# A recurrent attention and mixture-of-adapters kernel: batches one at a time, whole-tensor loads, five rotating PSUM banks

## The chip, the cores and the metric

The kernel runs on one core of a Trainium2 chip. The metric is device time in microseconds (us), the median of several executions. One execution is also taken by the hardware profiler; its span runs from the first to the last instruction of the program.

## What is computed

Four batches, eight heads, 768 steps, 48 columns per head, all in float32. A gated linear recurrence runs over the steps of each head; its output, seen as 3072 rows of 384, goes through a mixture of eight rank-16 adapters, of which the two with the highest gate logits are used:

```python
for t in range(S):
    state = alpha[:, :, t, :, None] * state + np.einsum('bhd,bhe->bhde', k[:, :, t], v[:, :, t])
    y[:, :, t] = np.einsum('bhd,bhde->bhe', q[:, :, t], state)
...
logits = x @ w_gate                      # x: y as (3072, 384)
topk = np.argpartition(-logits, K, axis=1)[:, :K]      # K = 2
...                                      # w: softmax over the two
    z = x[mask] @ A[e]
    delta[mask] += w[mask, k, None] * (z @ B[e])
return (x + delta).astype(np.float32)
```

## The kernel before, in words

**Units.** The steps are cut into chunks of 128, six for each batch, and a unit u (0 to 23) is one chunk of one batch with all eight heads: 128 rows on the partitions, 384 columns. `_place(u)` gives a unit its batch and chunk. Before, batches go in pairs: units 0, 2, 4 ... are batch 0 and units 1, 3, 5 ... batch 1, then the other two batches, so two recurrences advance in turn.

**Steps of a unit**, each a short function called with u:

- `ln` (ACT, L238): logarithm of alpha, for one unit or a pair of units (`LNS`); `cum` (PE, L244): sums of it over the chunk by a product with a triangle; `exp` (ACT, L255): two activations, exp of the sums and of their negative, into `ex`.
- `kg` (POOL, L260): k and q times those, one multiplication of 128 x 768 into `kgq`; `vb` (POOL, L265): v to bfloat16.
- `tr` (PE, L268): eight transposes of `kgq`; `kq` (ACT, L274): their copy to SBUF; `at` (PE, L280): eight products of k and q into `at_t`; `msk` (DVE, L288): times the causal mask, into `am`.
- `st` (DVE, L294): state of the chunk before, out of PSUM bank `S_t`, times the decay, into `sb`; `kv` (PE, L300): the new state, an identity product of `sb` and four products of k and v. The first chunk of a batch has no old state.
- `av` (PE, L314): the output, from `sb` and from `am`; `ysb` (ACT, L330): its copy into `o_t`.

**Adapters.** `xb` (POOL, even units), `xt` (PE), `xs` (ACT, L345) bring the output in transposed. Then the units go in groups (`GROUPS`, mostly three): `z` (PE) makes adapter products and logits, `gm df ge wu dn w zw` (DVE, L364 to L418) and `gx` (ACT) the two best, their weights and the weighted z, `zt` (PE) and `zs` (ACT) transpose it. `dl` (PE, L431) is the last product of a unit, `o` (DVE, L437; ACT for unit 23) adds it to `o_t`, and `out` stores 192 KB from SP's queue.

**The order** is written out by hand: each token of the string `ORDER` is a step, its unit or group, and for steps that write a rotating PSUM bank the bank's number (`MB` of them). Every engine runs its own steps in that order; so do the DMA queues. Loads stand among them: `Sk.4.2.exp3` is k on SP's ring from unit 4 on, two units, held until exp of unit 3 is done; `Aa.6.2` is alpha on ACT's ring, so it stands in ACT's own instruction stream. `w` loads are the weights. `load` (L150) turns a token into a DMA; one of two units is 384 KB (128 partitions x 16 rows of 192 B). The tiles `a_t`, `kq_t`, `v_t` have `NS` = 6 places, one for each pair of units, and `home` finds them. `cast_weights` (L211) brings the adapter weights to bfloat16 on DVE, at the token `cw`.

PSUM has eight banks: two for `at_t`, two for `S_t` (one for each of the two recurrences under way), four for the rotating `M_t`.

## Time and profile before

| | |
|---|---|
| median of 5 runs | 99.47 us (98.66 to 99.81) |
| the profiled execution | 99.19 us, span 97.5 us |
| busy, of the span | PE 71.8 (74%), DVE 68.0 (70%), ACT 67.2 (69%), POOL 61.2 (63%) |
| moved by DMA | 24.18 MB; HBM read 19.28 MB, written 4.72 MB |
| costliest groups | kg (L261) 24 x 1822 ns; msk (L289) 24 x 1215 ns; exp (L138) 48 x 507 ns; kq (L141) 24 x 593 ns |

PE is TensorE's matmuls and PEld its weight loads, DVE is VectorE, ACT ScalarE, POOL GpSimd, SP SyncE; ACTq and SPq are the DMA issues on the queues of ACT and SP. An idle time in brackets behind a row names what ended it. A slice of the page is a fortieth of the span, 2.4 us, and a digit the busy share in tenths. In the chain, each piece is what the next one waited for. An "x4" is a number of instructions put in one row.

### The profile page before, as it was taken

The page shows a single profiled execution, that of the slowest core. Times are in us where ns is not written, and L with a number is a line of the kernel's source. Part 1 is how long each engine was busy: PE and PEld are TensorE (multiplying, and loading weights), DVE is VectorE, ACT ScalarE, POOL GpSimd, SP SyncE. Part 2 cuts the span into 40 slices and gives each one's busy share as a digit, 9 for nine tenths or more (in the row PEclk, how much of TensorE's full clock was granted, in tenths as well). Part 3 has the DMA queues.
Part 4 walks back from the last instruction along what each step waited for, and adds up shares of the span by engine and source line. Part 5 has one row for each costly group of instructions (what it writes and reads, how often), then busy time and mean ns, then how long its engine had stood idle before and what let it go on. Part 6 is the DMA issues. An engine that isn't in the chain of part 4 may idle for free.

```text
span 97.5 us, 2861 instructions
## 1 busy us (share of the span) xinstructions
PE 71.8 (74%) x1088; PEld 54.8 (56%) x1088; DVE 68.0 (70%) x171; ACT 67.2 (69%) x155; POOL 61.2 (63%) x70
## 2 busy tenths in 40 slices
...
DMA  1999999999999999999999999999999989998553
GB/s 27 245 260 259 260 260 258 260 230 258 282 263 260 260 254 259 257 236 251 248 242 254 261 261 257 260 238 197 260 205 236 254 165 392 330 392 322 189 205 118
DMA packets 103966, 24.18 MB, mean 248 GB/s; under 512 B 100752, under 2 KB 103952, under 8 KB 103952
## 3 DMA queue, kind: packets, MB, share of 16 engines
...
HBM read 19.28 MB, written 4.72 MB: 246 GB/s over the span
## 4 chain that ended last, share of the span: by engine, by line
DMA 24%; DVE 22%; PE 21%; ACT 15%; POOL 8%; issue 5%; ACTq 1%; POOLq 0%; DVEq 0%
DMA kq_t<-in_q_dram 14%; POOL kgq L261 8%; DVE am L289 7%; DMA v_t<-in_v_dram 6%; DVE o_t L441 6%; ACT ex L138 5%; PE M_t L272 4%; ACT kt L141 4%; PE at_t L285 4%; DMA a_t<-in_alpha_dram 4%; PE M_t L246 3%; DVE w L405 2%; PE M_t L343 2%; ACT lg L138 2%; ACT xs L141 2%
## 5 line engine op out<-in xcount | busy, mean ns | idle before, releaser
L261 POOL TENSOR_TENSOR kgq<-kq_t,ex 128x768 bf16<-128x768 f32 x24 | 43.3, 1822 | 12.8 <-ACT xs L141 4.2
L289 DVE TENSOR_TENSOR am<-at_t,mask 128x1024 bf16<-128x1024 f32 x24 | 29.2, 1215 | 16.4 <-PE at_t L285 16.4
L138 ACT ACTIVATE ex<-M_t 128x392 f32<-128x392 f32 (+1 forms) x48 | 21.2, 507 | 3.0 <-PE M_t L250 3.0
L141 ACT COPY kt<-M_t 128x512 f32<-128x512 f32 x24 | 14.2, 593 | 6.8 <-PE M_t L272 6.5
L272 PE MATMUL M_t<-ident,kgq 128*128 128x128 bf16 x192 | 16.2, 234 | 3.6 <-POOL kgq L261 3.6
L266 POOL CAST vb<-v_t 128x384 bf16<-128x384 f32 x24 | 11.8, 506 | 10.5 <-DMA v_t<-in_v_dram 10.5
L141 ACT COPY o_t<-M_t 128x384 f32<-128x384 f32 x25 | 12.4, 495 | 5.5 <-PE M_t L326 4.8
L246 PE MATMUL M_t<-lg,suf 128*128 128x384 bf16 x24 | 8.9, 369 | 9.5 <-ACT lg L138 9.3
L272 PEld LDWEIGHTS <-kgq 128*128 128x128 bf16 x192 | 12.5, 105 | 5.1 <-POOL kgq L261 4.6
L295 DVE TENSOR_TENSOR sb<-S_t,ex 128x384 bf16<-128x384 f32 x20 | 10.8, 547 | 4.3 <-PE S_t L309 4.0
L441 DVE TENSOR_TENSOR o_t<-M_t,o_t 128x384 f32<-128x384 f32 x23 | 12.2, 546 | 1.6 <-PE M_t L434 1.2
L285 PE MATMUL at_t<-kt 48*128 48x128 bf16 x192 | 10.4, 233 | 2.5 <-ACT kt L141 1.9
L138 ACT ACTIVATE lg<-a_t 128x768 bf16<-128x768 f32 (+1 forms) x13 | 10.6, 813 | 2.4 <-DMA a_t<-in_alpha_dram 2.4
L326 PE MATMUL M_t<-vb,am 128*128 128x48 bf16 x192 | 9.1, 187 | 0.9 <-DVE am L289 0.7
L285 PEld LDWEIGHTS <-kt 48*128 48x128 bf16 x192 | 6.0, 99 | 5.8 <-ACT kt L141 3.6
L434 PE MATMUL M_t<-B_all,zs 128*128 128x384 bf16 x24 | 8.2, 356 | 1.2 <-ACT zs L141 1.2
L326 PEld LDWEIGHTS <-am 128*128 128x128 bf16 x192 | 7.3, 99 | 1.8 <-DVE am L289 1.4
L334 POOL CAST xb<-o_t 128x384 bf16<-128x384 f32 x12 | 6.1, 505 | 2.8 <-ACT o_t L141 2.8
L343 PE MATMUL M_t<-ident,o_t 128*128 128x128 f32 x36 | 7.3, 314 | 0.4 <-DVE mx L367 0.3
L141 ACT CAST xs<-M_t 128x384 bf16<-128x384 f32 x12 | 5.9, 494 | 2.3 <-PE M_t L343 2.3
L309 PE MATMUL S_t<-vb,kgq 128*128 128x96 bf16 x80 | 7.4, 220 | 0.1
L247 PEld LDWEIGHTS <-ident 128*128 128x128 bf16 x24 | 2.5, 102 | 8.2 <-issue 8.2
...
## 6 DMA issues: line engine op xcount, KB each, us to landing
...
```

Source lines behind the costliest of these rows:

```text
L138: recent[:] = [nc.scalar.activation(*args, **kw)]
L141: recent[:] = [nc.scalar.copy(*args)]
L246: nc.tensor.matmul(r[:, 0:DM], suf[:, :], t[:, :, 0:D], start=True, stop=True)
L261: nc.gpsimd.tensor_tensor(out=kgq[u % KEEP["kg"]][:, :, :, 0:D], in0=kq_t[u // 2 % NS][:, :, u % 2, :, 0:D], in1=ex[u % KEEP["ex"]][:, :, ...
L266: nc.gpsimd.tensor_copy(out=vbt[u % KEEP["vb"]], in_=home("v", u)[:, u % 2, :, 0:D])
L272: nc.tensor.transpose(t[:, w, p, :], pair(kgq[u % KEEP["kg"]][:, w], p), ident[:, :])
L285: nc.tensor.matmul(at_t[:, hh, p, :], kq[rows, 0, p, :], kq[rows, 1, p, :], start=True, stop=True)
L289: nc.vector.tensor_tensor(out=am[u % KEEP["am"]].rearrange("p a b t -> p (a b) t"), in0=at_t.rearrange("p a b t -> p (a b) t"), in1=_bc_mi ...
L295: nc.vector.tensor_tensor(out=sb[u % KEEP["sb"]].rearrange("p a b d -> p (a b) d"), in0=S_t[u % 2].rearrange("p a b d -> p (a b) d"), in1= ...
L326: nc.tensor.matmul(y[:, h * D:(h + 1) * D], am[u % KEEP["am"]][:, hh, p, :], vbt[u % KEEP["vb"]][:, h, :], start=(c == 0 and h == 0), stop ...
L343: nc.tensor.transpose(t[:, i * P:(i + 1) * P], x[:, i, :], idn[:, :])
L441: nc.vector.tensor_tensor(out=o_t[u], in0=bank("dl", u)[:, 0:DM], in1=o_t[u], op=ALU.add)
```

## The change

- `_place`: units 0 to 5 are batch 0, 6 to 11 batch 1, and so on. One recurrence is under way at a time, with one `S_t` bank; `MB` goes from four to five.
- `load`: a load takes one tensor of one batch whole (six units, 1152 KB; 128 partitions x 48 rows of 192 B), sixteen in all; alpha and q on SP's ring, k and v on ACT's. The tiles hold two batches, with the columns in the order head, chunk. The first tokens on ACT's queue are k of batch 0 and two weight loads, then ln.0, then v of batch 0.
- `ka`: for units 0 to 5 the multiplication of `kg` is made in two halves, k (`ka`) and q (`kg`), with separate places in the order.
- `cast_weights` runs on ACT. `xs` of even units copies the bfloat16 columns as 192 float32 words.
- `GROUPS` ends in 3, 2, 1 units instead of 2, 2, 1, 1 (nine groups for ten); `ex` has five tiles and `kgq` six, for four and four; `am` has four, for three.
- `ORDER` is written anew. The DVE steps from msk.18 to the last zw are 56 where they were 49; of `out`, six stand ahead of `vb.18`.

```diff
--- before.py
+++ after.py
@@ -28,57 +28,54 @@
 NEG = -30000.0
 
 
-GROUPS = [[0, 1, 2], [3, 4, 5], [6, 7, 8], [9, 10, 11], [12, 13, 14], [15, 16, 17], [18, 19], [20, 21], [22],
+GROUPS = [[0, 1, 2], [3, 4, 5], [6, 7, 8], [9, 10, 11], [12, 13, 14], [15, 16, 17], [18, 19, 20], [21, 22],
           [23]]
 LNS = [[0], [1]] + [[u, u + 1] for u in range(2, NU, 2)]
 CAST = set(range(0, NU, 2))
 HOLD = {23}
-KEEP = dict(lg=2, ex=4, kg=4, kt=4, am=3, sb=3, vb=4, xs=9, xb=3, mx=3, xe=3, wu=3, dn=3, w=3, zw=3, zs=3)
+SPLIT = {0, 1, 2, 3, 4, 5}
+KEEP = dict(lg=2, ex=5, kg=6, kt=4, am=4, sb=3, vb=4, xs=9, xb=3, mx=3, xe=3, wu=3, dn=3, w=3, zw=3, zs=3)
 NS = 6
-MB = 4
+MB = 5
 ORDER = """
-Sa.1.1 Aa.0.1 Sk.0.1 Aa.2.2 Sv.2.2 ln.0 Aq.0.1 cum.0.0 Sk.1.1.ln0 Sv.0.1.ln0 exp.0 Av.1.1 ln.1 Aq.1.1 cum.1.1 exp.1
-vb.2 kg.0 Ak.2.2 Sq.2.2.exp1 Sw.2.0 ln.2 cum.2.2 tr.0.3 vb.0 kq.0 kg.1 Aa.4.2 at.0 Sv.4.2.kq0 kv.0 msk.0 exp.2
...
-zt.4.0 tr.18.1 cum.21.2 zs.4 kq.18 dl.9.3 st.19 av.17.0 o.9 dl.13.1 Sv.22.1.kq18 vb.19 ysb.17 at.18 o.13 exp.21
-dl.12.3 xb.16 tr.19.0 msk.18 vb.18 xt.16.1 Av.20.2 kq.19 dl.14.2 Sv.23.1.exp21 kg.20 kv.19 xs.16 out.13 o.12 xt.17.0
-out.2 at.19 o.14 xs.17 av.18.1 msk.19 z.5.3 kg.21 ysb.18 out.1 ln.22 kv.18 gm.5 tr.20.2 ge.5 av.19.0 df.5 st.20 gx.5
-kq.20 xb.18 tr.21.1 wu.5 st.21 ysb.19 at.20 dn.5 kq.21 vb.20 w.5 xt.18.2 xt.19.0 msk.20 vb.21 xs.18 out.0 cum.22.1
-xs.19 cum.23.2 exp.22 z.6.0 zw.5 at.21 exp.23 gm.6 zt.5.3 msk.21 av.20.1 kg.22 out.11 zs.5 kv.21 ysb.20 dl.17.2
-dl.16.3 out.10 df.6 ge.6 av.21.1 o.17 gx.6 out.6 kv.20 wu.6 ysb.21 o.16 xb.20 out.4 tr.22.2 dn.6 kg.23 st.22 dl.15.1
-xt.21.3 kq.22 w.6 o.15 xs.21 at.22 zw.6 xt.20.2 out.12 msk.22 xs.20 zt.6.1 vb.22 tr.23.3 out.14 zs.6 z.7.0 out.15
-kq.23 dl.18.2 st.23 av.22.1 out.9 gm.7 at.23 o.18 ysb.22 out.7 dl.19.3 df.7 xb.22 msk.23 out.3 gx.7 vb.23 xt.22.1
-out.17 xs.22 ge.7 out.18 av.23.2 wu.7 o.19 z.8.1 out.16 ysb.23 dn.7 gm.8 w.7 out.19 xt.23.3 df.8 zw.7 gx.8 out.5
-wu.8 xs.23 zt.7.0 w.8 out.8 zs.7 z.9.3 zw.8 dl.20.0 gm.9 zt.8.1 df.9 o.20 gx.9 zs.8 dl.21.1 wu.9 out.20 dl.22.0 w.9
-zw.9 o.22 zt.9.3 o.21 zs.9 out.22 dl.23 out.21 o.23 out.23
+Sa.0.6 Ak.0.6 Sw.0.0 Aw.1.0 Sw.2.0 Sq.0.6 Sa.6.6 Sq.6.6 Aw.3.0 ln.0 Av.0.6 ln.1 cum.0.0 exp.0 cum.1.1 ln.2 exp.1
+cum.3.2 cum.2.3 exp.3 ka.1 exp.2 ka.3 ln.4 ka.0 kg.0 kg.1 tr.0.4 cum.4.0 kq.0 cum.5.1 kg.3 tr.1.2 at.0 kq.1 ka.2
+tr.3.3 msk.0 kq.3 kg.2 exp.4 at.1 msk.1 tr.2.4 Ak.6.6 exp.5 vb.0 kq.2 vb.1 kv.0 av.0.2 vb.2 st.1 at.2 ln.6 ka.5
+msk.2 av.1.3 kv.1 ln.8 kg.4 cum.7.0 cum.6.1 st.2 ysb.0 at.3 cw.0 ka.4 av.2.4 cum.9.2 kv.2 exp.6 kg.5 st.3 exp.7
+tr.4.1 msk.3 xb.0 vb.3 ysb.1 xt.0.0 ysb.2 tr.5.3 Av.6.6 xb.2 Sa.12.6.ysb2 kv.3 vb.4 kq.4 st.4 vb.5 kq.5 at.4
+Sq.12.6.kq4 ln.10 av.3.4 msk.4 kv.4 kg.6 ysb.3 cum.8.1 Sa.18.6.kq5 xs.0 xt.2.3 st.5 exp.9 xt.1.4 av.4.0 xs.2 at.5
+xs.1 kg.7 tr.6.2 msk.5 ysb.4 exp.8 z.0.3 xt.3.4 kq.6 gm.0 av.5.0 xs.3 xb.4 ge.0 df.0 tr.7.1 gx.0 kg.9 ysb.5 wu.0
+cum.11.2 kq.7 dn.0 xt.4.4 w.0 xt.5.0 xs.4 zw.0 at.6 Ak.12.6 cum.10.1 msk.6 zt.0.4 kg.8 xs.5 exp.11 z.1.3 tr.9.0 zs.0
+gm.1 exp.10 dl.1.2 vb.6 ge.1 tr.8.4 o.1 ln.12 vb.7 kv.6 df.1 at.7 vb.9 st.7 kq.9 cum.12.1 vb.8 msk.7 dl.2.2 kq.8
+av.6.0 kg.10 kv.7 gx.1 ysb.6 cum.13.4 ln.14 st.8 at.8 wu.1 o.2 kv.8 exp.12 dl.0.0 vb.10 st.9 tr.10.2 exp.13 xb.6
+msk.8 kv.9 kg.11 av.7.1 kq.10 cum.15.4 Av.12.6 st.10 av.8.2 ysb.7 dn.1 at.9 o.0 ysb.8 kv.10 vb.11 w.1 exp.15
+cum.14.1 msk.9 xb.8 tr.11.0 exp.14 xt.6.2 kg.12 Sq.18.6.exp15 xt.7.4 zw.1 at.10 kq.11 st.11 av.9.1 ln.16 msk.10
+zt.1.3 kg.13 zs.1 tr.12.0 xs.6 xs.7 dl.3.3 xt.8.2 at.11 o.3 xs.8 cum.16.4 kq.12 msk.11 z.2.2 kg.14 ysb.9 dl.4.3
+exp.16 av.10.0 gm.2 av.11.1 o.4 ysb.10 at.12 ysb.11 df.2 ge.2 kg.15 tr.13.4 msk.12 Ak.18.6 tr.14.0 gx.2 kq.13 dl.5.3
+cum.17.1 kq.14 wu.2 o.5 at.13 exp.17 xt.11.4 dn.2 msk.13 vb.12 xt.9.0 xs.11 xb.10 av.12.3 xs.9 vb.13 kv.12 w.2
+tr.15.1 ln.18 vb.14 st.13 at.14 kg.16 zw.2 kq.15 xt.10.4 cum.18.0 msk.14 xs.10 kv.13 exp.18 zt.2.2 z.3.1 zs.2 st.14
+vb.15 at.15 ysb.12 gm.3 dl.6.4 ln.20 xb.12 tr.16.0 msk.15 kg.17 av.13.2 kq.16 dl.7.3 kv.14 ysb.13 o.6 av.14.0
+Av.18.6 df.3 at.16 o.7 out.6 gx.3 ysb.14 cum.19.2 vb.17 out.2 st.15 tr.17.4 vb.16 exp.19 ge.3 msk.16 kv.15 xb.14
+cum.20.3 kq.17 kg.18 xt.13.0 exp.20 wu.3 st.16 at.17 dl.8.2 dn.3 xs.13 msk.17 cum.21.4 av.16.3 exp.21 kg.19 tr.18.0
+w.3 ysb.16 kv.16 o.8 kq.18 av.15.4 zw.3 xt.14.3 at.18 st.17 xs.14 kg.20 zt.3.2 ysb.15 xt.12.0 msk.18 tr.19.1 zs.3
+xs.12 dl.10.3 z.4.4 kq.19 o.10 ln.22 kg.21 at.19 gm.4 out.10 tr.20.2 msk.19 out.0 dl.9.0 av.17.1 kq.20 out.4
+cum.22.3 out.5 ysb.17 df.4 vb.18 dl.11.2 ge.4 o.9 out.1 at.20 gx.4 exp.22 vb.19 tr.21.1 wu.4 dn.4 xb.16 o.11 kv.18
+kq.21 xt.15.0 vb.21 w.4 av.18.3 st.19 xs.15 kg.22 xt.17.2 zw.4 ysb.18 xt.16.1 cum.23.0 xs.17 msk.20 zt.4.3 xs.16
+kv.19 zs.4 z.5.4 exp.23 vb.20 st.20 dl.13.2 xb.18 at.21 gm.5 kv.20 kg.23 o.13 av.20.1 ge.5 st.21 tr.22.3 ysb.20 df.5
+av.19.0 msk.21 gx.5 kv.21 vb.22 ysb.19 dl.12.2 tr.23.1 kq.22 xb.20 wu.5 st.22 xt.18.0 vb.23 at.22 o.12 xs.18 av.21.3
+kq.23 dn.5 msk.22 out.12 kv.22 ysb.21 out.11 xt.20.0 xt.19.2 out.3 xs.20 w.5 out.13 av.22.1 xs.19 st.23 out.9 at.23
+ysb.22 zw.5 xt.21.3 msk.23 xb.22 zt.5.0 xs.21 z.6.2 zs.5 dl.14.1 xt.22.4 gm.6 av.23.3 xs.22 o.14 dl.16.0 z.7.4 ge.6
+df.6 out.14 o.16 dl.15.1 gx.6 ysb.23 out.8 wu.6 gm.7 xt.23.0 out.7 dn.6 df.7 ge.7 w.6 gx.7 out.16 xs.23 wu.7 o.15
+dl.17.0 zw.6 z.8.1 out.15 gm.8 zt.6.2 dn.7 df.8 o.17 zs.6 gx.8 w.7 dl.18.2 out.17 wu.8 dl.20.0 o.18 zw.7 dl.19.2
+out.18 w.8 o.20 zt.7.4 zs.7 o.19 out.20 dl.21.0 dl.22.4 zw.8 out.19 o.21 zt.8.2 o.22 zs.8 out.21 dl.23 out.22 o.23
+out.23
 """
 
 
 
 def _place(u):
 
-    g, r = divmod(u, 2 * NCH)
-    return 2 * g + r % 2, r // 2
+    return divmod(u, NCH)
 
 
 def _bc(src: bass.AP, rep: int) -> bass.AP:
@@ -114,14 +111,16 @@
 
     SRC = dict(a=alpha, k=k, q=q, v=v)
     big.tile([P, 32], F4, name="row_start")
-    a_t = [big.tile([P, 2, H, HP], F4, name=f"a_t{i}") for i in range(NS)]
-    kq_t = [big.tile([P, 2, 2, H, HP], F4, name=f"kq_t{i}") for i in range(NS)]
-    v_t = [big.tile([P, 2, H, HP], F4, name=f"v_t{i}") for i in range(NS)]
+    a_t = [big.tile([P, NCH * H, HP], F4, name=f"a_t{i}") for i in range(2)]
+    kq_t = [big.tile([P, 2, NCH * H, HP], F4, name=f"kq_t{i}") for i in range(2)]
+    v_t = [big.tile([P, NCH * H, HP], F4, name=f"v_t{i}") for i in range(2)]
     o_t = [big.tile([P, DM], F4, name=f"o_t{u}") for u in range(NU)]
 
-    def home(x, u):
-        i = u // 2 % NS
-        return dict(a=a_t[i], k=kq_t[i][:, 0], q=kq_t[i][:, 1], v=v_t[i])[x]
+    def home(x, b):
+        return dict(a=a_t[b % 2], k=kq_t[b % 2][:, 0], q=kq_t[b % 2][:, 1], v=v_t[b % 2])[x]
+
+    def chunks(t):
+        return t.rearrange("p (h c) d -> p c h d", c=NCH)
 
     W_st = consts.tile([P, E, NF, R], F4, name="W_st")
     G_st = consts.tile([P, NF, E], F4, name="G_st")
@@ -153,9 +152,13 @@
             eng.dma_start(out=WSRC[u][0], in_=WSRC[u][1])
             return
         b, c = _place(u)
-        dst = home(x, u)[:, u % 2:u % 2 + n, :, 0:D].rearrange("p b h d -> p (b h) d")
-        dma = eng.dma_start(
-            out=dst, in_=SRC[x][b:b + n, :, c * C:(c + 1) * C, :].rearrange("b h j d -> j (b h) d"))
+        if n == NCH:
+            dma = eng.dma_start(out=home(x, b)[:, :, 0:D],
+                                in_=SRC[x][b].rearrange("h (c j) d -> j (h c) d", j=C))
+        else:
+            for i in range(c, c + n):
+                dma = eng.dma_start(out=chunks(home(x, b))[:, i, :, 0:D],
+                                    in_=SRC[x][b, :, i * C:(i + 1) * C, :].rearrange("h j d -> j h d"))
         if name:
             behind(dma, name[0])
 
@@ -209,14 +212,12 @@
     B_all = consts.tile([P, DM], F2, name="B_all")
 
     def cast_weights():
-        nc.vector.tensor_copy(
-            out=W[:, :, 0:E * R].rearrange("p i (e r) -> p e i r", e=E), in_=W_st)
-        nc.vector.tensor_copy(out=W[:, :, E * R:NZ], in_=G_st)
-        nc.vector.tensor_copy(out=B_all, in_=B_st)
+        nc.scalar.copy(W[:, :, 0:E * R].rearrange("p i (e r) -> p e i r", e=E), W_st[:, :, :, :])
+        nc.scalar.copy(W[:, :, E * R:NZ], G_st[:, :, :])
+        nc.scalar.copy(B_all[:, :], B_st[:, :])
 
     at_t = ps.tile([P, 2, NP, P], F4, name="at_t")
-    S_t = [ps.tile([P, 512], F4, name=f"S_t{i}")[:, 0:DM].rearrange("p (a b d) -> p a b d", a=NP, b=2)
-           for i in range(2)]
+    S_t = ps.tile([P, 512], F4, name="S_t")[:, 0:DM].rearrange("p (a b d) -> p a b d", a=NP, b=2)
     M_t = [ps.tile([P, 512], F4, name=f"M_t{i}") for i in range(MB)]
     lof = {u: (i, us.index(u)) for i, us in enumerate(LNS) for u in us}
     gof = {u: (g, us.index(u)) for g, us in enumerate(GROUPS) for u in us}
@@ -238,8 +239,9 @@
     def ln(u):
         i, _ = lof[u]
         n = len(LNS[i])
+        b, c = _place(u)
         act(lgs[i % KEEP["lg"]][:, 0:n, :, 0:D],
-                             home("a", u)[:, u % 2:u % 2 + n, :, 0:D], AF.Ln)
+            chunks(home("a", b))[:, c:c + n, :, 0:D], AF.Ln)
 
     def cum(u):
         t, r = lg(u), bank("cum", u)
@@ -257,13 +259,23 @@
         act(ex[u % KEEP["ex"]][:, 0, :], r[:, 0:DM + 2 * NP], AF.Exp)
         act(ex[u % KEEP["ex"]][:, 1, 0:DM], r[:, 0:DM], AF.Exp, scale=-1.0)
 
+    def scaled(u, part):
+        b, c = _place(u)
+        nc.gpsimd.tensor_tensor(
+            out=kgq[u % KEEP["kg"]][:, part, :, 0:D],
+            in0=kq_t[b % 2].rearrange("p w (h c) d -> p w c h d", c=NCH)[:, part, c, :, 0:D],
+            in1=ex[u % KEEP["ex"]][:, part, 0:DM].rearrange("p w (h d) -> p w h d", h=H), op=ALU.mult)
+
+    def ka(u):
+        scaled(u, slice(0, 1))
+
     def kg(u):
-        nc.gpsimd.tensor_tensor(
-            out=kgq[u % KEEP["kg"]][:, :, :, 0:D], in0=kq_t[u // 2 % NS][:, :, u % 2, :, 0:D],
-            in1=ex[u % KEEP["ex"]][:, :, 0:DM].rearrange("p w (h d) -> p w h d", h=H), op=ALU.mult)
+        part = slice(1, 2) if u in SPLIT else slice(0, 2)
+        scaled(u, part)
 
     def vb(u):
-        nc.gpsimd.tensor_copy(out=vbt[u % KEEP["vb"]], in_=home("v", u)[:, u % 2, :, 0:D])
+        b, c = _place(u)
+        nc.gpsimd.tensor_copy(out=vbt[u % KEEP["vb"]], in_=chunks(home("v", b))[:, c, :, 0:D])
 
     def tr(u):
         t = bank("tr", u).bitcast(F2).rearrange("p (w n s) -> p w n s", w=2, n=NP)
@@ -294,12 +306,12 @@
     def stf(u):
         nc.vector.tensor_tensor(
             out=sb[u % KEEP["sb"]].rearrange("p a b d -> p (a b) d"),
-            in0=S_t[u % 2].rearrange("p a b d -> p (a b) d"),
+            in0=S_t.rearrange("p a b d -> p (a b) d"),
             in1=_bc(ex[u % KEEP["ex"]][:, 0, DEC], D), op=ALU.mult)
 
     def kv(u):
         _, c = _place(u)
-        S = S_t[u % 2]
+        S = S_t
         if c:
             nc.tensor.matmul(
                 S.rearrange("p a b d -> p (a b d)"), ident[:, :],
@@ -343,8 +355,11 @@
             nc.tensor.transpose(t[:, i * P:(i + 1) * P], x[:, i, :], idn[:, :])
 
     def xs(u):
-        t = bank("xt", u).bitcast(F2) if u in CAST else bank("xt", u)
-        act_copy(xst[u % KEEP["xs"]].rearrange("p i t -> p (i t)"), t[:, 0:DM])
+        t, y = bank("xt", u), xst[u % KEEP["xs"]].rearrange("p i t -> p (i t)")
+        if u in CAST:
+            act_copy(y.bitcast(F4), t[:, 0:DM // 2])
+        else:
+            act_copy(y, t[:, 0:DM])
 
     def zv(g):
         n = len(GROUPS[g])
@@ -448,7 +463,7 @@
     def cw(_):
         cast_weights()
 
-    RUN = dict(ln=ln, cum=cum, exp=exp, kg=kg, vb=vb, tr=tr, kq=kq, at=at, msk=msk, st=stf, kv=kv,
+    RUN = dict(ln=ln, cum=cum, exp=exp, ka=ka, kg=kg, vb=vb, tr=tr, kq=kq, at=at, msk=msk, st=stf, kv=kv,
                av=av, ysb=ysb, xb=xb, xt=xt, xs=xs, z=z, gm=gm, df=df, ge=ge, gx=gx, wu=wu, dn=dn,
                w=w, zw=zw, zt=zt, zs=zs, dl=dl, o=o, out=store, cw=cw)
```

## The prediction

> **What bounds the kernel now.** I read the page first, then a table of stretches, the chain that ended last, and the timelines of SP, ACT and DVE. The page says how far the loads set the pace:
>
> ```profile
> span 97.5 us, 2861 instructions
> ...
> DMA  1999999999999999999999999999999989998553
> GB/s 27 245 260 259 260 260 258 260 230 258 282 263 260 260 254 259 257 236 251 248 242 254 261 261 257 260 238 197 260 205 236 254 165 392 330 392 322 189 205 118
> DMA packets 103966, 24.18 MB, mean 248 GB/s; under 512 B 100752, under 2 KB 103952, under 8 KB 103952
> ```
>
> The DMA engines are busy in every slice up to the stores, and the rate sits at 260 GB/s. It rises to 392 only where the 24 stores run: their rows are 1536 B long, the loads' rows 192 B (48 floats). The stretches show the engines beside it (columns: PE, PEld, DVE, ACT, POOL busy, granted clock, DMA share, GB/s):
>
> ```profile
> 55.00:60.00 5.00, 4.68 (x86) 3.53 (x86) 4.86 (x15) 4.82 (x13) 4.05 (x5) 1.00 1.28 259
> 60.00:65.00 5.00, 3.19 (x60) 2.54 (x58) 3.30 (x7) 3.04 (x8) 3.88 (x3) 1.00 1.28 260
> 65.00:70.00 5.00, 4.05 (x73) 3.33 (x68) 4.86 (x15) 4.76 (x12) 3.81 (x5) 1.00 1.08 219
> 70.00:75.00 5.00, 4.91 (x83) 3.94 (x84) 5.00 (x9) 3.60 (x9) 5.00 (x6) 1.00 1.10 221
> ```
>
> From 60 to 65 all engines thin out at 260 GB/s: they wait for data. From 65 on DVE is full and DMA is not: loads have got ahead, and DVE carries the end. The chain says so in order of time:
>
> ```profile
> 0.83 3.60 DMA a_t<-in_alpha_dram
> ...
> 34.58 6.12 DMA v_t<-in_v_dram
> 40.70 7.44 DMA kq_t<-in_q_dram
> ...
> 54.72 6.24 DMA kq_t<-in_q_dram
> ...
> 61.12 1.82 POOL kgq L261
> ...
> 62.98 0.64 PE M_t L272 x8
> ...
> 63.70 0.59 ACT kt L141
> ...
> 64.34 0.42 PE at_t L285 x8
> 64.78 1.03 DVE am L289
> ```
>
> Loads end the waits until 61, then one unit's steps follow, kg to tr to kq to at to the mask product: 3.7 us from kg's start (61.12) to the mask (64.78). After that DVE's own queue is the chain, in its timeline:
>
> ```profile
> 13.44 1.23 DVE L289 TENSOR_TENSOR am<-at_t,mask 128x1024 bf16<-128x1024 f32 x1 [11.35 <-PE at_t L285]
> ```
> ```profile
> 72.48 1.21 DVE L289 TENSOR_TENSOR am<-at_t,mask 128x1024 bf16<-128x1024 f32 x1
> ...
> 92.57 0.35 DVE L413 SCALAR_TENSOR_TENSOR zw<-M_t,dn,wu 128x128 bf16<-128x128 f32 x1
> ```
>
> The first mask product starts at 13.44. That at 72.48 is unit 18's, sixth from the last; from there to the end of the last zw (92.92) are 20.4 us, nearly without a hole, and from there to the span's end (97.5) 4.6 us (transpose, copy, last product, store). The profiled execution took 99.19 us, 1.7 more than its span, and 0.3 less than the median of 99.47. My sum is a span plus 1.7.
>
> **The loads, part by part.** A whole tensor of a batch is 128 x 48 rows of 192 B, 1.18 MB; the row length is not changed, so I take 260 GB/s; the ends are 221, what SP's ring moved nearly alone (row of 70 to 75), and the stores' 392. Sixteen such loads and 0.41 MB of weights are the 19.28 MB that the page has as read. What changes is which bytes come first.
>
> Head. Slice 0 (2.4 us at 27 GB/s) puts the first data at 2.2. The first alpha now shares the engines with k of the same batch: 2.36 MB at 260 is 9.1 us, and 0.4 from last data to signal (393 KB of first alphas moved by 3.7, the chain's landed at 4.43). ln.0 starts at 11.7 instead of 4.45, 7.2 later. q and v of batch 0 follow with the weights: 5.13 MB, 19.7 us, so q lands at about 21.7. Until then ACT runs ln 0 to 5 and exp 0 to 3, and POOL three of the k halves (half of 1822 ns, 0.9 each). Then kg.0 0.9, tr 1.05, kq 0.6, at 0.6 (rows of unit 0 in the trace): the first mask product at 25, instead of 13.44. DVE has nothing to do for 11.5 us more.
>
> Rings. k of batch 1 stands on ACT's queue behind exp.4, which needs the steps up to kq.3; by rows of 0.6 and 0.9 us that is near 26, first data 1.4 later. ACT's ring is empty from 21.9 to 27.4; SP's ring alone moves about 221 GB/s (the row of 70 to 75), so 15% of 5.5 us, 0.8, is lost. Later A loads have 13 to 16 ACT steps between them, about 8 us by their rows, against 9.1 us of a ring's half share: each is issued about when its ring runs dry. Bounds: no gap, or 2 us each on four loads, of which the other ring takes back most: 0 to 4. I take 0.6, near the low end, since SP's queue has its next load waiting throughout.
>
> Last loads. Unit 18 is the first of batch 3, and its kg needs all of k and q of that batch. Before, unit 18's needed only 384 KB pieces. Ahead of both in the rings are all but one of the tensors: 15 x 1.18 + 0.41 = 18.1 MB, 69.6 us at 260. So k and q of batch 3 land at 2.2 + 69.6 + 0.8 + 0.4 = 73.0.
>
> End. Unit 18's mask product then starts at 73.0 + 0.1 + 3.7 = 76.8, where before it was at 72.48. Behind it stand, in DVE's order to the last zw, the steps of before plus four o (0.46 each as they follow one another, 1.8), one st (0.5), and routing groups of 3,3,3,2,1 units for 3,2,2,1,1 (1.9, 1.7 and 1.0 us by the rows of their steps: plus 1.1): 20.4 + 3.4 = 23.8. Sum: 76.8 + 23.8 + 4.6 = 105.2, with the ring gaps 105.8; time 107.5. DVE can do no more in advance: its queue is in order, and all that stands ahead of that mask product (63.5 us in all, see rival 4, less 23.8: 40) fits in the 52 us since 25.
>
> v of batch 3, alone on the rings with six stores beside it: 1.18 MB at 221 is 5.3, the stores' 1.18 MB at 390 up to 3.0, so it lands at 78 to 82. Its first use on DVE's path, st.19, comes 5.2 us of DVE steps after 76.8, at 82.0; v plus vb (0.5) and kv (0.45) gives 79 to 83. Covered within 1 us. POOL: four kg of 1.82 from 73.0 end at 80.3, four casts, kg.22, two casts and kg.23 end at 86.9, and 13.7 more (83.8 to 97.5 before) is 100.6: below DVE.
>
> **The smaller edits.** Weight casts: 2.3 us (rows 1829, 164, 344 ns) leave DVE in a stage where it waits for batch 1 and saves nothing; on ACT they cost 1.2 (its copies of 384, 24 and 384 columns: 0.5, 0.2, 0.5) to 2.3 in the same wait, nothing on the path, that much if the wait were gone. xs as 192 words: 344 for 494 ns, 12 times, 1.8 us off ACT, off the path. A state bank less, and one state chain instead of two: a step is st 0.55, the identity product 0.35 and four products 0.43, 1.5 us with gaps against 4 us per unit; taken at 0, up to 3 if PE's queue stalls on it. A fifth bank, five ex and six kgq: nothing to a gain of 1, as waits on full buffers are not what ends the chain.
>
> A page for the change: the Trainium skill's "DMA: Bandwidth & Descriptors", section "Measured (HBM→SBUF, 128 partitions, SWDGE, issued from GpSimd)", gives 341 GB/s for transfers of 1 MB and asks for 1 MiB and more. By that figure the 18.1 MB would take 53 us, the batch 3 signal would come near 57, and the sum would be about 91. The same page's "Specifications" asks for 512 B or more per transfer for line rate, which the rows of 192 B stay under; this trace has 260 against 392 GB/s for the two row lengths, and at 384 KB no sign that a longer transfer of equal rows is faster.
>
> **Does the issue hold ACT?** The SP and ACT timelines:
>
> ```profile
> 9.08 0.47 SPq L157 DMA_DIRECT2D kq_t<-in_q_dram  x1
> 9.59 3.59 SPq L153 DMA_DIRECT2D G_st<-in_moe_w_gate_dram  x1
> ```
> ```profile
> 6.11 2.02 ACTq L157 DMA_DIRECT2D kq_t<-in_q_dram  x1
> ...
> 8.18 0.50 ACT L138 ACTIVATE ex<-M_t 128x392 f32<-128x392 f32 x1 [1.23 <-PE M_t L250]
> ```
>
> An issue on ACT's queue holds what is behind it: the exp could start at 7.6 and started at 8.18. But 384 KB were issued in 0.47 and the 12 KB after them in 3.59: an issue waits until the transfer before it has been taken in, its own size does not count. In the change A loads are 8 us or more apart, so each should take near 0.4.
>
> **The rivals.**
> 1. Faster: one mechanism, the load rate. Whole tensors might stream better than 260. To end under 98.5 the batch 3 signal must come 9 us sooner, at 64: 18.1 MB in 60.6 us, 298 GB/s. From there it decides; at 310 GB/s the signal is at 61 and the time near 96. For: the stores' 392. Against: the same 192 B rows, and 259 to 260 from the head, where pieces of 192 and 384 KB mix, to the middle, where all are 384.
> 2. ACT is held by its own issues: if 384 KB are taken at once and the rest at half of 260 GB/s, 770 KB hold ACT 6 us. Six such after the head are 36; ACT (67.2 busy, some 8 of it done by 25) has 23 us idle between 25 and 107 to hide in, so 13 to 36 more, about 125. Against: the 0.47 and 3.59 above; for: no issue of 1.18 MB was ever seen.
> 3. Rings run dry: ACT reaches the A loads later than I have it, and with 2 us lost net per load the batch 3 signal slips by 4 to 8: 111 to 116. For: k of batch 1 waits on ACT already, and 65 to 80 of this trace runs at 210 to 220.
> 4. The order does not bring its waits (loads hidden anyway): then DVE runs from 25 without a hole: 68.0 busy less 1.2 of early memsets, 2.3 of casts and 1 of group steps is 63.5; with 4.6 that ends at 93, and with holes like those of 65 to 90 (2%) the time is 95 to 97. Against: 18.1 MB cannot land before 72 at 260.
>
> **How the numbers follow.** My forecast (104 to 111): 0.55. Rings dry (111 to 118): 0.20. ACT held (over 118): 0.08. Smaller losses than I have, 100.5 to 104: 0.06. Same within 1%, which is about what a measurement of this kernel can tell from no change: 0.04. Faster, rivals 1 and 4: 0.07. So slower 0.89. The range leaves out the held case and the faster ones: 101 to 117; the forecast's own is 104 to 111.
>
> **What would show it.** Right: rate at 260 from 5 to 20; ln.0 near 11.7; the first mask product near 25; kg.18 released by a load near 73; DVE then full to 5 us before the end; ACT's issues at 0.4. Wrong: a rate over 295 in the load stretch (rival 1); issues of 4 to 6 us on ACT (rival 2); a DMA share falling well under 1.28 between 27 and 72 (rival 3); or kg.18 released by an engine and not by a load.

## The result and the profile after

The changed kernel takes 100.18 us (median of 44 executions, 98.85 to 101.71), the kernel before 99.39 (79 executions in the same sessions, 98.55 to 101.11): a ratio of 1.0048, 95% interval 1.0028 to 1.0068. The forecast was 107.5, range 101 to 117. So a large change moved the time by half a per cent, and the prediction of a slower kernel was wrong. The profiled execution took 99.42 us with a span of 97.7. Times of one session are compared by their ratio to the kernel before in that session. The ratios leave out executions more than 1.5% above the fastest of their kernel, so they can differ from the quotient of the medians, which count every execution; in e15 that leaves only the profiled one, so its rows are used and not its time.

Line numbers are now those of the changed kernel: L264 is the product of `kg` and `ka`, L301 the mask product, L420 `w`, L432 `zw`. The page of the changed kernel answers first to the rate:

```profile
span 97.7 us, 2788 instructions
...
DVE  5000000036726767879998999999999999999930
...
GB/s 0 253 314 313 308 311 329 317 317 210 298 305 276 236 314 309 316 317 316 310 315 315 312 317 315 210 143 330 180 113 286 13 0 7 203 277 320 165 321 85
DMA packets 29645, 24.17 MB, mean 247 GB/s; under 512 B 1856, under 2 KB 29632, under 8 KB 29632
```

The loads run near 314 GB/s, not 260, and the packets have changed with the rate: there were 103966, now 29645. Of those from 512 B to 2 KB (29632 less 1856), the 24 stores are 3072 rows of 1536 B and one weight 128; 24576 are left for sixteen loads, 1536 each, so 768 B apiece: four rows of 192 B. A row of one head lies behind its neighbour in memory, on another partition in SBUF; that the DMA reads four such rows at once and spreads them over four partitions is inferred from this count. The DVE row shows the rest of the story: empty for seven slices after the first, thin for the next ten, then full to the end. The same in stretches (columns: PE, PEld, DVE, ACT, POOL busy, granted clock, DMA share, GB/s):

```profile
20.00:25.00 5.00, 4.50 (x55) 3.61 (x55) 2.98 (x3) 3.51 (x9) 4.36 (x8) 1.00 0.90 255
25.00:30.00 5.00, 5.00 (x70) 3.75 (x65) 1.81 (x3) 4.78 (x13) 3.69 (x5) 1.00 1.06 311
30.00:35.00 5.00, 4.63 (x76) 4.04 (x75) 3.94 (x5) 3.28 (x9) 3.27 (x5) 1.00 0.93 256
...
45.00:50.00 5.00, 4.89 (x86) 4.02 (x82) 4.93 (x12) 4.72 (x14) 4.66 (x7) 1.00 1.08 314
...
60.00:65.00 5.00, 5.00 (x98) 4.25 (x96) 5.00 (x12) 4.56 (x13) 5.00 (x7) 1.00 0.71 183
```

The stage where all engines used to thin out for data (60 to 65) is full now; the thin one is 20 to 45, where DVE is idle 7.1 us after its first mask product. DVE's timeline, with the first mask products of batch 0 and batch 1, then unit 18's:

```profile
21.19 1.23 DVE L301 TENSOR_TENSOR am<-at_t,mask 128x1024 bf16<-128x1024 f32 x1 [18.81 <-PE at_t L297]
...
39.53 1.21 DVE L301 TENSOR_TENSOR am<-at_t,mask 128x1024 bf16<-128x1024 f32 x1
...
67.20 1.50 DVE L420 TENSOR_TENSOR w<-wu,dn 128x24 f32<-128x24 f32 x1
...
70.03 1.21 DVE L301 TENSOR_TENSOR am<-at_t,mask 128x1024 bf16<-128x1024 f32 x1
...
92.53 0.34 DVE L428 SCALAR_TENSOR_TENSOR zw<-M_t,dn,wu 128x128 bf16<-128x128 f32 x1
```

Unit 18's mask product starts at 70.03, 2.45 earlier than in the kernel before (72.48). From it to the end of the last zw (92.87) are 22.84 us for 20.44, 2.4 more, and from there to the end of the span 4.8 for 4.6. That is the whole account: the 2.45 us won up to unit 18 are given back, 2.40 of them behind unit 18. There the new order has the longer list of DVE steps, and one `w` takes 1.60 us where the slowest of the kernel before took 0.88 (at 83.00), which is 0.7 of the 2.40. POOL's timeline shows what let unit 18 start (its kg is the first of the four at 65.06; k of batch 3 had landed at 64.27, so POOL's own casts and not the load released it):

```profile
61.93 1.83 POOL L264 TENSOR_TENSOR kgq<-kq_t,ex 128x768 bf16<-128x768 f32 x1
63.70 0.96 POOL L278 CAST vb<-v_t 128x384 bf16<-128x384 f32 x2
64.59 0.51 POOL L346 CAST xb<-o_t 128x384 bf16<-128x384 f32 x1
65.06 7.16 POOL L264 TENSOR_TENSOR kgq<-kq_t,ex 128x768 bf16<-128x768 f32 x4
```

And the issues on ACT's and SP's queues, where the prediction expected 0.4 us:

```profile
1.79 8.41 ACTq L152 DMA_DIRECT2D W_st<-in_moe_A_dram  x1
...
38.27 1.97 ACTq L156 DMA_DIRECT2D kq_t<-in_k_dram  x1
```
```profile
14.78 7.86 SPq L156 DMA_DIRECT2D kq_t<-in_q_dram  x1
```

A 96 KB weight load behind a whole tensor was held for 8.41 us, so ln.0, whose alpha had landed at 9.87, started at 10.81. The later loads on ACT's queue take 0.70 us where the load ahead of them has landed or lands within 2.4 us, and 1.21 to 2.67 where it has 3.0 to 4.0 us to go. They hold ACT too: its copy for unit 4 started at 31.80, right behind an issue that lasted from 29.03 to 31.70, although its transposes were done at 30.88.

### The profile page after: what moved, and what is told of

Same layout as the page of the kernel before. It is cut to its first block, busy times and chain, and to the rows that moved or that the text cites. A ratio compares the mean times of both kernels' runs of the same rounds, so it can differ in the third digit from the quotient of the medians.

```text
span 97.7 us, 2788 instructions
## 1 busy us (share of the span) xinstructions
PE 70.5 (72%) x1088; PEld 55.2 (57%) x1088; DVE 65.8 (67%) x165; ACT 64.5 (66%) x164; POOL 61.7 (63%) x76
## 2 busy tenths in 40 slices
DMA packets 29645, 24.17 MB, mean 247 GB/s; under 512 B 1856, under 2 KB 29632, under 8 KB 29632
## 4 chain that ended last, share of the span: by engine, by line
DVE 30%; PE 15%; POOL 12%; ACT 12%; DMA 11%; ACTq 11%; issue 6%; POOLq 0%
DMA kq_t<-in_k_dram 11%; DVE am L301 10%; POOL kgq L264 10%; ACTq L152 9%; DVE o_t L456 6%; DVE sb L307 5%; ACT ex L137 4%; PE M_t L284 3%; DVE zw L432 3%; PE at_t L297 2%; ACT o_t L140 2%; DVE w L420 2%; ACT lg L137 2%; POOL vb L278 2%; ACT kt L140 2%
## 5 line engine op out<-in xcount | busy, mean ns | idle before, releaser
L264 POOL TENSOR_TENSOR kgq<-kq_t,ex 128x768 bf16<-128x768 f32 (+1 forms) x30 | 44.0, 1495 | 16.7 <-ACT ex L137 14.8
L301 DVE TENSOR_TENSOR am<-at_t,mask 128x1024 bf16<-128x1024 f32 x24 | 29.1, 1213 | 20.9 <-PE at_t L297 20.9
L284 PE MATMUL M_t<-ident,kgq 128*128 128x128 bf16 x192 | 17.0, 239 | 3.3 <-POOL kgq L264 3.3
L284 PEld LDWEIGHTS <-kgq 128*128 128x128 bf16 x192 | 13.0, 107 | 5.1 <-POOL kgq L264 4.1
L278 POOL CAST vb<-v_t 128x384 bf16<-128x384 f32 x24 | 11.6, 507 | 2.0 <-DMA v_t<-in_v_dram 1.3
L355 PE MATMUL M_t<-ident,o_t 128*128 128x128 f32 x36 | 6.8, 303 | 0.5 <-ACT o_t L140 0.4
```

What stands on the lines that cost most here:

```text
L264: nc.gpsimd.tensor_tensor(out=kgq[u % KEEP["kg"]][:, part, :, 0:D], in0=kq_t[b % 2].rearrange("p w (h c) d -> p w c h d", c=NCH)[:, part, ...
L278: nc.gpsimd.tensor_copy(out=vbt[u % KEEP["vb"]], in_=chunks(home("v", b))[:, c, :, 0:D])
L284: nc.tensor.transpose(t[:, w, p, :], pair(kgq[u % KEEP["kg"]][:, w], p), ident[:, :])
L301: nc.vector.tensor_tensor(out=am[u % KEEP["am"]].rearrange("p a b t -> p (a b) t"), in0=at_t.rearrange("p a b t -> p (a b) t"), in1=_bc_mi ...
```

## The experiments

Theory A: the failed step is the load rate; at 260 GB/s the rest of the sum would have held. Its second half says what holds the kernel at 97.7 in spite of the rate: the late first products and the landing of batch 1. Rivals: the new DVE order or the smaller edits made up for slower loads, or the issues on ACT set the pace.

**e1: the old rate.** Each whole load is cut in two, one head and seven heads; the loads' order and bytes stay.

```diff
-            dma = eng.dma_start(out=home(x, b)[:, :, 0:D],
-                                in_=SRC[x][b].rearrange("h (c j) d -> j (h c) d", j=C))
+            for lo, hi in ((0, 1), (1, H)):
+                dma = eng.dma_start(out=home(x, b)[:, lo * NCH:hi * NCH, 0:D],
+                                    in_=SRC[x][b, lo:hi].rearrange("h (c j) d -> j (h c) d", j=C))
```

> Each of the sixteen whole loads is cut in two on the same queue, one head (6 rows of 192 B per partition) and seven heads (42 rows, 1008 KB); same bytes, same order, nothing else. Theory A (only the rate of my sum was wrong): if the cut brings back packets of 192 B and 260 GB/s, k and q of batch 3 land near 72 to 74 instead of 64.3 and 61.0, unit 18's mask product starts near 77 instead of 70.0, and the time is 104 to 109 against 100.2 for the changed kernel. Theory B (the engines set the end, the loads are hidden at either rate): 99.5 to 102, although the loads land later. If the packets stay at 768 B: no change, and the run tells nothing on the rate.

Measured: 110.02 us, ratio 1.106 (1.099 to 1.112). From its page:

```profile
GB/s 32 248 261 261 280 262 261 261 260 252 222 259 261 260 261 262 256 261 260 259 260 260 258 260 261 260 236 276 258 83 262 111 1 0 102 320 314 149 296 69
DMA packets 103629, 24.17 MB, mean 224 GB/s; under 512 B 100416, under 2 KB 103616, under 8 KB 103616
```

Pieces of 1008 KB go in 192 B packets at 260 GB/s, the whole 1152 KB in 768 B packets at 314. With the old rate the kernel does what the prediction said: first mask product at 25.26 (25 predicted), q and k of batch 3 landing at 72.4 and 74.1 (73.0), unit 18's mask product at 79.16 (76.8), time 110.0 (107.5; a little over the 104 to 109 that theory A gave e1). Theory A's first half is shown; the loads gain ten per cent, and the rest of the change costs them. Not quite all of the ten is the rate, since e1 also has twice as many issues (ACT stood idle 3.31 us behind one, until 37.20). That the larger packet makes the rate is read from the two going together: 192 B and 260, 768 B and 314, the stores' 1536 B and 392.

**e2: a warm TensorE; e4: another order of the first products; e7: both.** In e2, 171 matmuls into a bank whose contents nobody reads stand between the first steps. In e4, `ka.0` comes first and `at.0` ahead of `tr.1`.

```diff
+    def wm(n):
+        for _ in range(n):
+            nc.tensor.matmul(M_t[4][:, 0:P], suf[:, :], suf[:, :], start=True, stop=True)
...
-... exp.3 ka.1 exp.2 ka.3 ln.4 ka.0 kg.0 kg.1 tr.0.4 cum.4.0 kq.0 cum.5.1 kg.3 tr.1.2 at.0 kq.1 ...
+... exp.3 ka.0 exp.2 ka.1 ln.4 ka.3 kg.0 kg.1 tr.0.4 cum.4.0 kq.0 at.0 cum.5.1 kg.3 tr.1.2 kq.1 ...
```

> The changed kernel with 171 added matmuls of the triangle by itself in the head, while PE waits for alpha and q; they go into a bank that tr.0 overwrites and nobody reads them. Theory C (PE is slow after its long idle head and lies on the path at 24.7 to 31.2): in the changed kernel the 384-column cum rows take 478 to 527 ns until 29 and about 325 from 33 on; with the added work they should take about 325 from the first, the stretch from the first mask to 31 should shrink by 2 to 3 us, and the time should fall to 97 to 98.5. Rival: loads of batch 1 and DVE's queue take it back later; then within 0.5 us of the changed kernel.

> Order alone: POOL makes ka.0 before ka.1 and ka.3 (it waited for exp of unit 1 until 14.24 although exp of unit 0 was done at 13.0), and PE makes at.0 before tr.1. Theory D (the head counts one for one): the first mask product moves from 21.2 to about 20 and the time falls by 0.5 to 1.2. Rival: the steps of the other five units of batch 0 and the landing of batch 1's k at 33 set the pace, so within 0.3 us of the changed kernel.

> The added matmuls in the head and the new order of ka and at together. If both gains are separate (2.4 and 1.3 of the ratio of the two runs alone): 95.5 to 96.5. If both come from the same place, what follows the landing of batch 1 near 33: no better than the better one, 97 to 98.

Measured: e2 97.34 us, ratio 0.978 (0.969 to 0.986), in the range expected, but mostly not for the reason given. The 384-column cum did take 0.32 to 0.33 us up to 19 (0.48 to 0.53 in the changed kernel), but 0.42 to 0.49 again from 25.8 to 28, where the granted clock had fallen to 0.50, and the stretch from the first mask product to unit 3's did not shrink (9.75 us for 9.35). e4 98.39, 0.986 (0.980 to 0.992), somewhat more than expected; e7 98.02, 0.983 (0.973 to 0.994). The gains do not add. In e7 the first mask product is 1.8 us earlier than in the changed kernel, unit 15's 1.5 (59.82 for 61.32), the last 3.4. That gains grow behind unit 15 is not the head's doing; e10 finds what is.

**e3: the weight loads behind q of batch 0,** all on SP, so that nothing holds ACT's queue.

```diff
-Sa.0.6 Ak.0.6 Sw.0.0 Aw.1.0 Sw.2.0 Sq.0.6 Sa.6.6 Sq.6.6 Aw.3.0 ln.0
+Sa.0.6 Ak.0.6 Sq.0.6 Sw.0.0 Sw.1.0 Sw.2.0 Sw.3.0 Sa.6.6 Sq.6.6 ln.0
```

> The two weight loads leave ACT's queue and go to SP's, all four behind q of batch 0. In the changed kernel their issues held ACT from 1.79 to 10.76 and ln.0 began at 10.81, although alpha had landed at 9.87. Theory D (the head counts one for one): ln.0 near 10.0, q of batch 0 lands 0.3 to 0.8 earlier as less stands ahead of it, and the time falls by 0.5 to 1. Rival: a wait further on (q's landing, batch 1's loads) takes it back, within 0.3 us of the changed kernel.

Measured: 101.21 us, ratio 1.016 (1.011 to 1.022): a miss. ln.0 and q of batch 0 came 1.2 and 1.1 us earlier, the first mask product at 19.86, but q of batch 1 landed at 33.0 instead of 31.3, TensorE ran out of work (one hole of 2.3 us, from 32.65 to 34.95), and then ran at half clock. Stretches of e3, columns as above:

```profile
32.00:34.00 2.00, 0.65 (x19) 0.43 (x16) 1.28 (x2) 2.00 (x6) 0.92 (x1) 1.00 1.09 318
34.00:36.00 2.00, 1.05 (x14) 1.06 (x15) 0.00 (x0) 0.42 (x2) 2.00 (x2) 0.86 1.08 308
36.00:38.00 2.00, 2.00 (x25) 1.94 (x23) 0.85 (x6) 0.87 (x4) 2.00 (x3) 0.50 1.02 296
```

msk.6 started at 40.07, later than without the edit. The earlier start met the next load's landing and was worth nothing; how much of the loss comes from q's later landing and how much from the clock, no run separates.

**e5: less DVE work.** `o` adds only the first 192 of 384 columns, so half of the output lacks the adapters' part.

```diff
-out=o_t[u], in0=bank("dl", u)[:, 0:DM], in1=o_t[u]
+out=o_t[u][:, 0:DM // 2], in0=bank("dl", u)[:, 0:DM // 2], in1=o_t[u][:, 0:DM // 2]
```

> The changed kernel, in which the step o adds only the first 192 of 384 columns; the adapter term of the other 192 is left out. Theory E (from 45 on DVE sets the end): an o is 0.46 us of DVE's time as they follow one another, half the columns save about 0.2, 21 of the 23 lie behind 45, so 4 us less work and a time of 95.5 to 97.5 against 100.2. Rival: PE or ACT stands right behind DVE and takes its place; then 99 to 100.5.

Measured: 97.31 us, ratio 0.982 (0.971 to 0.993), in the range. From unit 18's mask product to the end of the last zw are 20.01 us for 22.84. Of these 2.83 us, 1.42 are a `w` that took 0.18 (at 74.24) for 1.60, which the edit was not meant to change; the other 1.4 are the shorter `o`, so DVE's list is on the path, and worth about half of what the run gained.

**e6: fewer bytes in the kernel before.** v of units 12 to 23 is not loaded (they are computed with the v that lay in the same tiles): 2.36 MB less.

```diff
-... kv.9 xb.8 zs.1 Av.12.2 kg.11 ...          (and six more)
+... kv.9 xb.8 zs.1 kg.11 ...
```

> The kernel before, without the loads of v for units 12 to 23 (they compute with the v of units 0 to 11, so half of the output is of other data): 2.36 of 18.87 MB, 12.5% of the loads, as if they ran near 297 GB/s. Theory F (in the order of before the loads carry the time until about 61, so that order would have gained from a higher rate, where the changed order spends it on its late head): 95 to 97.5 against 99.4. Rival: DVE's queue carries the order of before whatever the loads do; 98.8 to 99.8.

Measured: 97.63 us, ratio 0.983 (0.974 to 0.992), just short of what was expected: 9 us less to transfer at 260 GB/s gain 1.7 us. Part of that is `w` again: unit 16's mask product came 0.66 us earlier (64.12 for 64.78), and the `w` behind it took 0.18 (at 67.36) for 1.09. Even in the kernel before, DVE stands close behind the loads.

**e8: the casts of the weights back on DVE.**

```diff
-        nc.scalar.copy(W[:, :, 0:E * R]..., W_st[:, :, :, :])     (and two more)
+        nc.vector.tensor_copy(out=W[:, :, 0:E * R]..., in_=W_st)  (and two more)
```

> The weight casts go back from ACT to DVE, all else as changed. My prediction costed this edit at nothing, since DVE waits for data in that stage (holes of 2.65 and 0.4 us near 27 to 32 in the changed kernel): within 0.5 us of 100.2. Rival: DVE's 2.3 us of casts delay st and msk behind them and DVE sets the end: 101 to 102.5.

Measured: 99.64 us, ratio 1.006 (1.002 to 1.010), span 97.6: no difference, as the prediction costed it.

**e10 and e12: `w` without two operands in SBUF.** The rows first: of the eight `w` of the changed kernel the last three took 0.17 to 0.18 us, the first three 0.32 to 0.63, and the two between them 1.50 (at 67.20, above) and 1.60 (at 74.71). POOL ran its four products from 65.06 on beside the first of these two, and one from 74.45 to 76.27 beside the second.

```profile
74.71 1.60 DVE L420 TENSOR_TENSOR w<-wu,dn 128x24 f32<-128x24 f32 x1
...
77.16 1.21 DVE L301 TENSOR_TENSOR am<-at_t,mask 128x1024 bf16<-128x1024 f32 x1
```
```profile
74.45 1.82 POOL L264 TENSOR_TENSOR kgq<-kq_t,ex 128x768 bf16<-128x768 f32 x1 [0.42 <-ACT ex L137]
```

In e10 `wu` stays in z's PSUM bank, so `w` reads one operand there; e12 is the same in the kernel before.

```diff
-nc.vector.tensor_tensor(out=wut[g % KEEP["wu"]][:, 0:n, :], in0=scratch(g, 1), ...)
+nc.vector.tensor_tensor(out=scratch(g, 0), in0=scratch(g, 1), ...)
...
-nc.vector.tensor_tensor(out=wt[g % KEEP["w"]][:, 0:n, :], in0=wut[g % KEEP["wu"]][:, 0:n, :], ...)
+nc.vector.tensor_tensor(out=wt[g % KEEP["w"]][:, 0:n, :], in0=scratch(g, 0), ...)
```

> The gate's weighted exponentials (wu) are kept in the PSUM bank of z and not in SBUF, so that w reads one operand from PSUM; nothing else changes. Theory: w's long instructions (1.50 us at 67.2, 1.60 at 74.7, 0.18 otherwise) are waits of VectorE for a GpSimd product that runs at that time and come with both of w's operands lying in SBUF; they go, msk.20 starts 1.5 us earlier than 77.16 after msk.18, and with VectorE bound to the end the time falls by 1.5 to 2.5 us, to 0.975 to 0.99 of the kernel before. Rival 1: they stay, since w still reads or writes SBUF while GpSimd runs: time within 0.3% of the changed kernel's. Rival 2: they go, but what they hid is waited for by the next mask product: the same time with idle time instead.

> The kernel before with w read from PSUM alone. Its two long w (1.09 us at 68.01, 0.88 at 83.00) are 1.6 us over the 0.18 of the others. If VectorE sets the end there: 0.985 to 0.99. If the last loads (landing at 81.1) or the masks that wait on them set it: the first is hidden and only the second counts, 0.99 to 1.0.

Measured: e10 97.78 us, ratio 0.981 (0.975 to 0.988), 2.4 points under the changed kernel; e12 97.66, 0.984 (0.979 to 0.988), a little more than either of its cases. In e10 the `w` at 67.17, in the middle of POOL's four products (65.05 to 72.20), where the changed kernel's took 1.50:

```profile
67.17 0.18 DVE L420 TENSOR_TENSOR w<-M_t,dn 128x24 f32<-128x24 f32 x1
...
68.79 1.23 DVE L301 TENSOR_TENSOR am<-at_t,mask 128x1024 bf16<-128x1024 f32 x1
```
```profile
65.05 7.15 POOL L264 TENSOR_TENSOR kgq<-kq_t,ex 128x768 bf16<-128x768 f32 x4
```

The next `w` of e10 (0.18 at 73.70) was over before its product began at 73.97, so it does not bear on this; in e12 the `w` at 67.79 took 0.18 within products that ran from 66.98 to 70.58. The last mask product of e10 came 2.4 us earlier (82.25 for 84.67). The Trainium skill's page "SBUF — State Buffer", section "SBUF: two separate sides", has a rule for it: a VectorE instruction with two SBUF inputs and a GpSimd instruction that reads SBUF lock each other out for the whole instruction. The rows agree: a `w` that starts within a product ends with it (76.31 and 76.27), and one that started within a POOL cast ended with that (48.81 and 48.78). In e2, e4 and e7 these two `w` happened to fall so that they took 0.2 to 0.6 us instead of 1.5 and 1.6. By unit 15's mask product e2 was 0.57 us ahead of the changed kernel and e4 0.39, by the last one 2.1 and 1.8: most of their gain came in the stretch where `w` waited less, not in the head.

**e9, e11, e18: batch 1 ahead of the weights.** In e9 the weights follow q of batch 1, k of batch 1 is issued right behind `kq.0`, and the casts wait until `xs.0`; e11 has e2, e4, e9 and e10 together; e18 is e9 and e10 with the casts just ahead of `z.0`.

```diff
-Sa.0.6 Ak.0.6 Sw.0.0 Aw.1.0 Sw.2.0 Sq.0.6 Sa.6.6 Sq.6.6 Aw.3.0 ln.0
+Sa.0.6 Ak.0.6 Sq.0.6 Sa.6.6 Sq.6.6 Sw.0.0 Sw.1.0 Sw.2.0 Sw.3.0 ln.0
...
-... kq.0 cum.5.1 ... tr.2.4 Ak.6.6 exp.5 ... at.3 cw.0 ka.4 ... Sa.18.6.kq5 xs.0 ...
+... kq.0 Ak.6.6 cum.5.1 ... tr.2.4 exp.5 ... at.3 ka.4 ... Sa.18.6.kq5 cw.0 xs.0 ...
```

> The four weight loads go to SP behind q of batch 1, k of batch 1 is issued right behind the eviction kq.0, and the casts wait until xs.0. Theory A with its second half (the late head and the landing of batch 1 set when DVE fills): k and q of batch 1 no longer stand behind the weights, so they land near 31 us instead of 33.0 and 31.3, msk.6 starts near 38 instead of 39.5, and the time is 1 to 1.5% under the changed kernel's, 0.985 to 0.995 of the kernel before. The rival (the earlier data finds TensorE throttled or the engines no readier, as in the run that moved the weights behind q of batch 0): msk.6 within 0.5 us of 39.5 and a time within 0.3% of the changed kernel's, or above it.

> The kernel with the warm TensorE (171 added matmuls whose results nobody reads), k's product of chunk 0 first, batch 1's loads ahead of the weights, and w from PSUM, all at once. If the four act on different stretches, they add in part: 0.96 to 0.975 of the kernel before. If each frees only what another holds again (as with warm and reorder together, 0.983 where the sum was 0.968): 0.975 to 0.985.

> The four weight loads behind q of batch 1 on SP, k of batch 1 right behind kq.0, the casts just ahead of the first product with the weights (z.0) and so behind the work of ScalarE that held them in the earlier run, and w read from PSUM. All of the reference is computed. If batch 1's landing gates and the weights (landing near 36.4) no longer hold ScalarE: the first product of batch 1 near 31.1 as before, msk.6 near 38, 0.97 to 0.98 of the kernel before (w alone: 0.981). If the weights are now late for z.0, whose maxima stand ahead of later mask products on VectorE: 0.985 to 1.03.

Measured: e9 104.93 us, ratio 1.051 (1.044 to 1.058); e11 100.97, 1.011 (1.006 to 1.016); e18 98.62, 0.987 (0.982 to 0.991). e9 and e11 miss; e18 lies in its second case, the late weights. In e9 the first product of batch 1 did start at 31.06 instead of 33.14, but ACT, whose order is fixed, stood behind the weights:

```profile
36.38 0.51 ACT L215 CAST W<-W_st 128x384 bf16<-128x384 f32 x1 [5.01 <-DMA W_st<-in_moe_A_dram]
```

In e18 ACT waits less, and DVE waits instead, in order behind the maxima of the first group:

```profile
37.96 0.32 DVE L382 MAX8 mx<-M_t 128x8 f32<-128x8 f32 x3 [4.08 <-PE M_t L376]
...
41.36 1.23 DVE L301 TENSOR_TENSOR am<-at_t,mask 128x1024 bf16<-128x1024 f32 x1 [0.80 <-PE at_t L297]
```

The edit moved the wait from one load to another (the weights, for q and k of batch 1). e9 alone could not say whether batch 1's landing gates, so e15 takes bytes away instead.

**e15 and e17: no alpha of batch 1.** Batch 1 is computed with batch 0's alpha; 1.18 MB less ahead of its q and k. e17 has e10 as well.

```diff
-Sq.0.6 Sa.6.6 Sq.6.6
+Sq.0.6 Sq.6.6
...
-        return dict(a=a_t[b % 2], ...
+        return dict(a=a_t[b == 2], ...
```

> alpha of batch 1 is not loaded; batch 1 is computed with the alpha of batch 0, so its output is not the reference's. This takes 1.18 MB, 3.75 us at 314 GB/s, from ahead of q and k of batch 1 and nothing from the engines. If the landing of batch 1 gates: its k and q land 2 to 3.7 us earlier than 33.0 and 31.3, msk.6 starts 1.5 to 3 us earlier than 39.5, and the time falls by 1 to 2.5 us, to 0.98 to 0.995 of the kernel before. If the late first products, TensorE's clock or the engines' order gate it: msk.6 within 0.5 us of 39.5 and a time within 0.3% of the changed kernel's.

> The kernel without alpha of batch 1 (its output is not the reference's), with w read from PSUM as well. Without alpha 1, GpSimd's first product of batch 1 started at 31.20 instead of 33.14 and msk.6 at 37.59 instead of 39.53, but only its profiled execution was shorter (span 94.5; the other three 98.4 to 98.8, at a lower clock). If batch 1's landing sets when VectorE is full, the gain over w alone (0.981, msk.6 at 40.33, last mask product at 82.25) is 1 to 2.5 us here: last mask product near 80, 0.955 to 0.975 of the kernel before. If the earlier start is lost again in the executions as a whole: 0.975 to 0.99.

Measured: e15 shows msk.6 at 37.59 for 39.53 and a span of 94.5 in the profiled execution (96.22 us), but the median of four is 100.12, which left the time open. e17 97.03 us, ratio 0.971 (0.966 to 0.975), in the range of its first case, against 0.981 (0.975 to 0.988) for e10; but its last mask product came at 81.57 and not near 80. Batch 1's landing does gate, but little: against e10, msk.6 of e17 is 3.1 us earlier (37.22), unit 15's 2.3, and the last one 0.7. What takes it back stands in e17's DVE timeline:

```profile
68.11 1.23 DVE L301 TENSOR_TENSOR am<-at_t,mask 128x1024 bf16<-128x1024 f32 x1 [0.32 <-PE at_t L297]
```

That is unit 18 again, 4.6 us behind unit 17 (63.47), waiting.

**e13, e14, e16: w from PSUM with warm, with the new order, and with both.**

> Warm TensorE (171 added matmuls whose results nobody reads) and w read from PSUM. Reading of the runs so far: of the 2.1 us by which the warm kernel's last mask product came earlier than the changed kernel's, only 0.57 us were there by msk.15 (60.75 against 61.32); the rest is that its w fell beside shorter products of GpSimd and waited 0.51 and 0.36 us, not 1.50 and 1.60. By that, warm and w from PSUM share most of their gain: last mask product near 81.7 (82.25 with w alone, less 0.57), 0.970 to 0.98 of the kernel before. If the two gains were independent (2.7% and 2.3% under the changed kernel): last mask product near 80.1, 0.95 to 0.96.

> k's product of chunk 0 first, and w from PSUM. By msk.15 reorder alone was 0.39 us ahead of the changed kernel (60.93 against 61.32): last mask product near 81.9, 0.97 to 0.983 of the kernel before. If it lies at 82.25 or later, reorder is worth nothing without w's waits, and all of its 1.8% was w.

> Warm TensorE, k's product of chunk 0 first, and w from PSUM, with the loads as in the changed kernel. By msk.15 warm and reorder together were 1.5 us ahead of the changed kernel (59.82 against 61.32), and w's two long waits are worth 2.4 us; if these add: last mask product near 80.75, 0.96 to 0.975 of the kernel before. If reorder's earlier products find VectorE or TensorE no readier: like warm and w alone.

Measured: e13 97.94 us, ratio 0.975 (0.964 to 0.987), last mask product at 81.87, as expected; e14 99.07, 0.986 (0.981 to 0.991), last one at 82.65, the second case: without w's waits the new order is worth nothing. e16 97.08, 0.976 (0.970 to 0.982), last one at 82.12 for 80.75: no better than e13, which is its second case, though not for the reason given there. The reason is in e16's POOL and DVE timelines:

```profile
64.93 7.16 POOL L264 TENSOR_TENSOR kgq<-kq_t,ex 128x768 bf16<-128x768 f32 x4 [1.36 <-DMA kq_t<-in_q_dram]
```
```profile
67.79 0.56 DVE L307 TENSOR_TENSOR sb<-S_t,ex 128x384 bf16<-128x384 f32 x1 [1.03 <-PE S_t L321]
68.67 1.23 DVE L301 TENSOR_TENSOR am<-at_t,mask 128x1024 bf16<-128x1024 f32 x1 [0.32 <-PE at_t L297]
```

POOL waits for q of batch 3, and unit 18's mask product follows kg's start by 3.74 us. In e13 (kg at 64.68, mask product at 68.41), e17 (64.38 and 68.11) and e14 (65.44 and 69.19) kg also starts within 0.1 us of q's landing; in e10 (65.05 and 68.79) it follows POOL's own casts, as in the changed kernel. With kg where it is there, DVE ahead of unit 18 can be helped by 1.2 us (70.03 to 68.80) and no more; beyond that the last batch's landing gates, which is the prediction's own mechanism at another time. e7, whose q landed near 63.9, had that mask product at 67.67. Nine of these kernels compute all of the reference and lie under the kernel before by their intervals: e2, e4, e7, e10, e12, e13, e14, e16 and e18. e2, e13 and e16 are the lowest, and their intervals overlap too far to rank them.

## Why the prediction was wrong, step by step

- "The row length is not changed, so I take 260 GB/s": this step failed, and alone decided the sign. What changed with it was the packet: a load of 1152 KB is moved in packets of 768 B, not 192. Measured: 314 GB/s; with the loads cut to 1008 and 144 KB, 260 again, and 110.0 us (e1). The page "DMA: Bandwidth & Descriptors", section "Measured (HBM→SBUF, 128 partitions, SWDGE, issued from GpSimd)", was weighed in the prediction and set aside for the row of 384 KB loads; its rule of 1 MiB and more pointed the right way here, by a step in the packet size that this section does not state. Its 341 GB/s for 1 MB stand against 314 here for 1152 KB and 260 in e1, where seven eighths of each tensor went in pieces of 1008 KB.
- "k and q of batch 3 land at 73.0": 64.3 and 61.0. 18.1 MB at 314 without a gap would be 2.2 + 57.6 + 0.4 = 60.2, so the rings lost about 4.1 us, not the 0.8 and 0.6 of the sum (255 GB/s from 20 to 25, where v of batch 0 has landed at 21.55 and k of batch 1 is issued at 22.14; 256 from 30 to 35; 183 from 60 to 65).
- "76.8 = 73.0 + 0.1 + 3.7": the 3.7 was exact (3.73 to 3.75 in five runs). With 64.3 it gives 68.1; measured 70.03, as POOL started kg.18 0.8 us after the landing and DVE was 1.2 behind through `w`'s wait of 1.50 at 67.20. That wait stood in the trace of before too (1.09 at 68.01) and was not seen. With it came one of the prediction's own signs of being wrong: kg.18 was released by its engine and not by a load.
- "20.4 + 3.4 = 23.8": 22.84. `w`'s waits are 1.42 of that, and 0.70 of the 20.44 of before; without them the longer list costs 1.7 us and not 3.4. "4.6": 4.8. With the measured landing the sum is 68.1 + 23.8 + 4.6 + 1.7 = 98.2, for 99.42 profiled.
- "The first mask product at 25": 21.19, by the rate (e1: 25.26). ln.0 at 11.7: 10.81, held by its own queue, not by the data.
- "That much fits in the 52 us since 25": 41 us of DVE work from 21.19 to 70.03, 48.8 us. It did fit, but of the 7.8 us of slack 7.1 went in holes before 45, which the prediction did not look at: it asked of no load but the last batch's what waits for it. e17 shows batch 1's landing to be worth 3.1 us at unit 6 and 0.7 at the end.
- The casts at nothing: shown (e8). v of batch 3 covered: it landed at 70.3. ACT's issues near 0.4: 0.70 free and up to 2.67 held, and 8.41 in the head. The prediction had read from its rows of 0.47 and 3.59 that an issue waits for the transfer before it, and did not put that to the weight loads right behind k of batch 0. Ahead of ln.0 they set the start; the later ones held ACT in the stage where DVE was thin, and what that cost no run separates. Moving the weights off ACT's queue gained nothing (e3).
- Rival 1 had the mechanism and the threshold, a signal at 64 for a time under 98.5. The signal came at 64.3, the time at 99.4. Its chance, with rival 4's, was 0.07; it deserved more, since the only row against it was one of loads a third as long. What came out, the same within 1%, had 0.04.

What stays open: why four rows are read together in loads of 48 rows per partition (1152 KB) and not in those of 42, 16 or 6. Whether the size decides or the number of rows, no run tells.
